# Units 0 to 3 of a delta-rule attention kernel: V summed in a PSUM bank instead of on VectorE, and four pieces' exponents made by ScalarE ahead of time

## The chip, the cores and the metric

The kernel runs on one core of a Trainium2 chip. The metric is device microseconds of one execution; a median over runs of the same program is given. The core has five instruction queues that matter here: TensorE (PE, matmuls into PSUM), VectorE (DVE), ScalarE (ACT), GpSimd (POOL) and SyncE (SP, which only issues DMAs). ScalarE and GpSimd issue a few DMAs too. Each works through its own instructions in program order and waits at semaphores for the others.

## The reference

Two blocks in a row. First a delta-rule attention over 4 batches x 8 heads, 768 steps, head dimension 48; then a feed-forward block on its 3072 rows of 384 features.

```python
k_n = k / (norm(k, axis=-1) + 1e-06)
for t in range(S):
    y[:, :, t] = einsum('bhd,bhde->bhe', q[:, :, t], state)
    v_old      = einsum('bhde,bhd->bhe', state, k_n[:, :, t])
    state     += beta[:, :, t] * outer(k_n[:, :, t], v[:, :, t] - v_old)
h = x @ w_in                       # 384 -> 2048
out = (h * sigmoid(1.702 * h)) @ w_out   # 2048 -> 384
```

q, k, v and beta arrive as 32-bit floats. The weights w_in and w_out arrive as 64-bit floats; the kernel reads them as pairs of 32-bit words and makes 32-bit floats of them with integer and float operations.

## The kernel before

**Units.** The sequence is cut into 6 chunks of 128 steps. The first chunk gives four units, 0 to 3, one for each batch; units 4 to 23 take two half chunks each (class Half). For a unit the recurrence becomes: a Gram matrix G = K K^T per head (gram_whole, line 475, for units 0 to 3), scores M = K Q^T (scores, 657), the triangular inverse of I + beta G in 32x32 diagonal blocks (invert, 543, on VectorE, for all of a chunk's units at once), a solve with it, and outputs and a state update (outputs, 768).

**The solve of units 0 to 3** goes over the four 32-row blocks of V. For each block, solve (716) multiplies V's block with the inverted diagonal block into psU, and solved (723) copies psU back over V as U, on ScalarE. Then below (703) multiplies Gram blocks with U into psR for every block further down, and rest (712) subtracts psR from V, on VectorE: for the first block in two instructions, rows 32 to 64 and the rest, for the others in one. together (1137) issues solves and belows of two units head by head in one burst. hops (1303) staggers two units so that one's solve runs beside the other's below: eight steps for units 0 and 1 (path), eight for 2 and 3 (later). warm(n) puts n matmuls without use on TensorE between the hops; put_out (1311) issues a unit's outputs and its state sum (line 766, ST<-psY,ST on VectorE).

**Conversion of the weights** is VectorE's work beside all this. conversion (224) is a generator. For one piece it does: mask the exponent (first operation, VectorE), rescale it (a Relu on ScalarE), put the sign in, mask the high mantissa, add the low word, multiply (four more on VectorE). pieces (249) gives the order: w_in in nine pieces, namely two halves of the first quarter (P0, P1), two of the second (P2, P3), three thirds of the third (P4 to P6), two halves of the last (P7, P8), 768 elements a partition each, but 512 for the thirds; then w_out in pieces of 384 or 768. conversions (275) overlaps neighbours: the next piece's first operation stands between the second and the third of the present one's, and its Relu is issued after it. fill(us) (322) pulls operations until their nominal costs (0.75, 0.95, 0.7, 0.95, 0.95) use up its budget; this writes VectorE's order by hand. After the piece of w_out that begins at block 6 the same stream goes on with the second inverse, invert(1), then with the rest of w_out. The last quarter of w_in is fetched into the place of P0 and P1, as soon as P1 is done (301), on SyncE's queue.

**The first inverse.** invert(0) runs on VectorE from 28.6 to 58.4 us. Beside it stand, in program order: the scores of units 0 to 3 (1285), the scaling of K of units 4 and 5 by 16 ScalarE instructions (next(scaling), 1290), their turns and Grams (1291 to 1294), then the rest of the inverse (1295). Its end puts 38 warming matmuls on TensorE (606) and sends the result through DRAM: stores Yd for units 0 and 1 on SyncE, for units 2 and 3 on ScalarE's queue (beside, 618), and loads XB for all four on SyncE (626). Behind them on SyncE: the diagonal blocks of units 4 and 5 (send_blocks), one piece of w_out, and inside the fill at 1301 the last quarter of w_in.

**After the solves** TensorE gets the feed-forward block: hidden (938), fed one step per hop from the fourth later hop on and then in the loop at 1382, together with fill(1.0); both_written (1084), which waits for converted w_out; and from unit 4 on slots (1186), in which the pending feed-forward work is spread between the small steps.

**PSUM** has eight banks: two for the feed-forward block (ps_moe), two "big", four "seq" until early_banks closes. A tile that takes a bank again waits for the readers of the tile before it.

```python
def rest(self, blk, psR):
    for u in (slice(BS, 2*BS), slice(2*BS, C)) if blk == 0 else (slice((blk+1)*BS, C),):
        vec.tensor_tensor(self.V[u], self.V[u], psR[u], op=ALU.subtract)
...
for i in range(2 * NB):
    together(*next(path))
    ...
    if 0 < i < 2 * NB - 1:
        fill(1.7)
```

Of the kernel before, what the change touches and what calls it, by code (L numbers as in the profile page):

```python
# [10 lines left out]
U32 = mybir.dt.uint32  # L11
AX = mybir.AxisListType
# [6 lines left out]
def kernel(  # L19
# [23 lines left out]
    C = 128  # L43
# [29 lines left out]
    ps_seq = early_banks.enter_context(tc.tile_pool(name="ps_seq", bufs=4, space=PSUM))  # L73
# [68 lines left out]
    bI = cpool.tile([128, BS], F32, name="bI")  # L142
    bL = cpool.tile([128, NC - 1, BS], F32, name="bL")
# [21 lines left out]
    pool.memset(low, -896.0 * (1 << 23))  # L165
    raws = w_out.rearrange("p f d -> p (f d)").bitcast(I32)
# [57 lines left out]
    def conversion(dst, raw, shape):  # L224
# [48 lines left out]
    done = set()  # L273

    def conversions():

        whole = list(pieces())

        def begin(i):
            dst, raw, shape, name = whole[i]  # L280
            ops = conversion(dst, places[name[1]] if raw is None else raw, shape)
            return ops, next(ops)
# [192 lines left out]
    def gram_whole(n):  # L475
# [7 lines left out]
        pool_, tag = (ps_seq, "seq") if c == 0 or n > DEEP + B else (ps_big, "big")  # L483
# [59 lines left out]
    def invert(c, b0=0, nb=B):  # L543
# [6 lines left out]
        tt(N, N, bc, op=ALU.mult)  # L550
# [88 lines left out]
    class Step:  # L639
# [62 lines left out]

        def below(self, blk, h, psR):
            r = slice(blk * BS, (blk + 1) * BS)
            for k in range(blk + 1, NB):
                u = slice(k * BS, (k + 1) * BS)
                pe.matmul(
                    psR[u, h, :], lhsT=self.G[r, h, u], rhs=self.U[r, h, :],
                    start=True, stop=True,
                )  # L710

        def rest(self, blk, psR):
            for u in (slice(BS, 2 * BS), slice(2 * BS, C)) if blk == 0 else (slice((blk + 1) * BS, C),):
                vec.tensor_tensor(self.V[u], self.V[u], psR[u], op=ALU.subtract)
# [24 lines left out]
        def queries(self):  # L739
            whole = [bank("psY", (128, 512)) for _ in range(2)]  # L740
# [396 lines left out]
    def together(solves, belows):  # L1137
# [4 lines left out]
        psRs = [bank("psR", big=blk == NB - 2 and len(belows) > 1) for X, blk in belows]  # L1142
# [106 lines left out]
    fetch_in(0, other_queue)  # L1249

# [15 lines left out]
    fetch_in(1, other_queue)  # L1266
    for b in range(B):
        load_values(b, sync)
    fetch_in(2)
# [15 lines left out]
    for s in pair:  # L1285
# [30 lines left out]
    path, later = hops(*pair[:2]), hops(*pair[2:])  # L1316
    for i in range(2 * NB):
# [31 lines left out]
    for i in range(1, 2 * NB):  # L1349
# [5 lines left out]
        fill(1.7)  # L1355
# [92 lines left out]
```

## Time and profile before

| | us |
|---|---|
| median of 3 runs | 719.43 (719.0 to 720.79) |
| profiled execution | 719.79 |
| its span, first to last instruction | 718.1 |
| PE / PEld busy | 673.8 / 580.2 |
| DVE busy | 464.8 |
| ACT / POOL busy | 232.8 / 252.3 |
| mean granted TensorE clock | 0.976 |

Times in the text are microseconds from the start of the span. A row of a timeline gives start, duration, engine, line, operation, output<-inputs by the program's names, shape, how many alike in a row, and in brackets how long the engine stood idle before it and who ended that. Most instructions carry line 122, where a helper records them: the names tell them apart. VU is V (and U over it), NT and YB the inverse's matrices, ph and po the two products of the feed-forward block, raw or w_out<-in_moe_w_in weights that are fetched (w_out's memory holds raw w_in for a while). A row with q behind the engine is a DMA issue by that queue. A busy TensorE is not TensorE at its peak, since a matmul's end is modelled.

| stretch | what runs |
|---|---|
| 0 to 28 | K, Grams of units 0 to 3, first piece of w_in |
| 28.6 to 58.4 | first inverse on VectorE |
| 64 to 84 | path: hops of units 0 and 1 |
| 83 to 109 | later: hops of units 2 and 3 |
| 101 to 149 | ph of the first rows; second inverse on VectorE from 123 to 154 |
| 161 to 718 | slots from unit 4 on |

### The profile page before, as it was taken

To read this page: it belongs to the slowest core of one execution; us is meant where nothing else is said; L and a number is where in the kernel's file an instruction comes from. 1 tells how busy PE (TensorE), PEld (TensorE's weight loads), DVE (VectorE), ACT (ScalarE), POOL (GpSimd) and SP (SyncE) were. 2 spreads that over 40 slices of the span, in tenths; PEclk is the share of its full clock that TensorE was granted. 3 is DMA by queue.
4 is the path that set the end of the run, shared out by engine and by line. 5 is a ranking of instruction groups with operands and counts; after the bars stand their busy time and mean duration, and the time that the engine had idled before them with its cause. 6 is when DMAs were issued, how large, how long until landed. Compare 5 with 4: busy or idle time off the path is not lost.

```text
span 718.1 us, 20437 instructions
## 1 busy us (share of the span) xinstructions
PE 673.8 (94%) x8779; PEld 580.2 (81%) x8779; DVE 464.8 (65%) x880; ACT 232.8 (32%) x553; POOL 252.3 (35%) x258
## 2 busy tenths in 40 slices
PE   9188899987999999999999999999999999999997
PEld 7156778853568888898988998988988988989997
DVE  5799988976577498597596695795893992110000
ACT  3362545433233313323333233323323223122020
POOL 6084003210256552552732633623522403304032
PEclk9577999999999999999999999999999999999999
DMA  9895845242222213214114123213122101000100
GB/s 169 143 187 112 215 126 134 56 79 81 57 52 60 57 37 79 42 37 94 29 37 92 31 57 73 46 44 60 33 53 57 29 24 32 8 23 2 28 0 23
DMA packets 129180, 46.66 MB, mean 65 GB/s; under 512 B 118849, under 2 KB 123585, under 8 KB 129089
## 3 DMA queue, kind: packets, MB, share of 16 engines
q1 hardware_dynamic: 125664, 40.94, 27.7%
q0 software_dynamic: 2240, 4.02, 2.8%
q8 instruction: 69, 1.13, 0.7%
q10 hardware_dynamic: 1184, 0.39, 0.2%
q14 instruction: 23, 0.18, 0.1%
HBM read 33.13 MB, written 11.01 MB: 61 GB/s over the span
## 4 chain that ended last, share of the span: by engine, by line
PE 52%; DVE 32%; DMA 7%; issue 4%; ACT 3%; SPq 2%; DVEq 0%; POOL 0%; ACTq 0%; POOLq 0%
PE ph L122 23%; PE po L122 17%; DVE P L122 12%; DVE YB L122 6%; PE four L122 4%; DVE NT L122 3%; DVE w_out L122 3%; DVE VU L122 3%; DMA NT<-Nd 2%; DMA Nd<-G 2%; PE psU L122 2%; PE psT L122 2%; PE ps_warm L122 2%; PE psR L122 2%; DVE w_in L122 1%
## 5 line engine op out<-in xcount | busy, mean ns | idle before, releaser
L122 PE MATMUL ph<-xT,w_in 128*128 128x256 f32 x1152 | 258.1, 381 | 0.2
L122 PEld LDWEIGHTS ph<-xT,w_in 128*128 128x128 f32 x1152 | 215.6, 190 | 30.6 <-DVE o L122 0.7
L122 PE MATMUL po<-w_out,gT 128*128 128x192 f32 (+1 forms) x720 | 139.7, 349 | 11.1 <-DVE w_out L122 5.4
L971 POOL TENSOR_TENSOR gT<-gT 128x512 f32<-128x512 f32 x80 | 105.1, 1323 | 103.6 <-ACT gT L122 68.4
L122 PEld LDWEIGHTS po<-w_out,gT 128*128 128x128 f32 x720 | 118.4, 191 | 25.5 <-DVE w_out L122 8.7
L122 DVE TENSOR_TENSOR P<-NT,YB 64x2 f32<-64x2 f32 (+9 forms) x200 | 121.4, 607 | 5.8
L122 ACT ACTIVATE gT<-ph 128x512 f32<-128x512 f32 x90 | 53.7, 597 | 144.9 <-PE ph L122 143.8
L122 DVE TENSOR_REDUCE YB<-P 64x2 f32<-64x2 f32 (+9 forms) x200 | 81.8, 409 | 6.9
L122 PE MATMUL po<-TW,gT 128*128 128x192 f32 x480 | 82.3, 328 | 1.1 <-ACT o L122 1.1
L122 PEld LDWEIGHTS po<-TW,gT 128*128 128x128 f32 x480 | 78.0, 190 | 2.4 <-ACT o L122 1.7
L122 ACT COPY VU<-psU 32x384 f32<-32x384 f32 x96 | 45.1, 470 | 58.5 <-PE psU L122 43.7
L839 POOL TENSOR_SCALAR_AFFINE_SELECT M<-M 64x512 f32<-64x512 f32 x40 | 30.0, 750 | 93.7 <-ACT M L122 91.7
L122 DVE TENSOR_TENSOR o<-o,po 128x192 f32<-128x192 f32 x40 | 13.9, 347 | 74.0 <-PE po L122 44.5
L122 DVE TENSOR_TENSOR VU<-VU,psR 32x384 f32<-32x384 f32 (+1 forms) x56 | 31.0, 554 | 41.7 <-PE psR L122 40.5
L122 DVE TENSOR_TENSOR NT<-NT,bL 64x1024 f32<-64x1024 f32 (+1 forms) x9 | 12.7, 1416 | 46.6 <-DMA NT<-Nd 46.6
L106 POOL DMA_DIRECT2D KN<-in_k_dram x24 | 17.1, 713 | 68.7 <-PE four L122 68.7
L122 DVE TENSOR_TENSOR VU<-VU,four 128x384 f32<-128x384 f32 x19 | 10.5, 551 | 45.7 <-issue 33.1
L122 PEld LDWEIGHTS psU<-VU,XB 32*32 32x32 f32 x1536 | 27.1, 105 | 15.0 <-issue 8.5
L341 POOL TENSOR_TENSOR rn<-ssq,half 128x8 f32<-128x8 f32 x12 | 22.2, 1849 | 45.7 <-DVE ssq L122 45.7
L122 ACT COPY xT<-four 128x256 f32<-128x256 f32 (+1 forms) x40 | 13.1, 328 | 74.5 <-DVE ST L122 72.1
L122 ACT COPY M<-four 128x512 f32<-128x512 f32 x19 | 11.1, 586 | 78.2 <-DVE VU L122 69.4
L122 PE MATMUL psU<-VU,XB 32*32 32x48 f32 x1536 | 32.0, 202 | 4.1 <-DVE VU L122 4.0
(123 smaller groups left out, 772.1 us busy)
## 6 DMA issues: line engine op xcount, KB each, us to landing
QP<-in_q_dram SPq DMA_DIRECT2D x40, 96.0 KB, 2.9
VU<-in_v_dram SPq DMA_DIRECT2D x40, 96.0 KB, 3.6
out_dram<-o SPq DMA_DIRECT2D x40, 96.0 KB, 2.2
raw<-in_moe_w_out_dram SPq DMA_DIRECT2D x9, 384.0 KB, 3.9
NT<-Nd SPq DMA_DIRECT2D x24, 128.0 KB, 2.4
XB<-Yd SPq DMA_DIRECT2D x24, 128.0 KB, 2.6
Yd<-NT SPq DMA_DIRECT2D x22, 128.0 KB, 2.2
Nd<-G SPq DMA_DIRECT2D x86, 32.0 KB, 1.7
```

The lines of the kernel that those rows point to most:

```text
L106: dma(out=place(dst, n)[rows, :, 0:D], in_=src[b, :, t, :].rearrange("h p d -> p h d"),)
L122: return lambda *a, **kw: tc.keep_in_program_order(op(*a, **kw))
L341: nc.gpsimd.tensor_tensor(rn, ssq, half, op=ALU.pow)
L839: nc.gpsimd.affine_select(out=M, in_=M, compare_op=ALU.is_gt, fill=0.0, base=0, pattern=[[0, H], [1, CH]], channel_multiplier=-1,)
L971: (engine or nc.gpsimd).tensor_tensor(o, a, b, op=op)
```

## The change

V of units 0 to 3 no longer lies in SBUF alone. gather starts a PSUM tile psV with V itself (a product with the identity); every below adds into it, for which the Gram is stored negated (bN, the negated beta, makes up for it in the first inverse); rest only copies the next 32 rows of psV to V, on ScalarE. The sixteen VectorE subtractions go, twelve ScalarE copies and four identity products come. The banks are dealt out anew: "seq" keeps two, two become "acc" (psV, and Grams and psY of odd units); psY of even units takes both of "seq".

For pieces P2 to P5 exponents makes the exponent on ScalarE alone, by three activations (Abs, a Relu on the upper 16 bits, a Relu), between the scores and after the Grams of units 4 and 5. The raw thirds of w_in are fetched ahead of V. In the hops the budgets and the warming are dealt out anew, and put_out of unit 0 comes after the last path hop.

```diff
-    ps_seq = early_banks.enter_context(tc.tile_pool(name="ps_seq", bufs=4, space=PSUM))
+    ps_seq = early_banks.enter_context(tc.tile_pool(name="ps_seq", bufs=2, space=PSUM))
+    ps_acc = early_banks.enter_context(tc.tile_pool(name="ps_acc", bufs=2, space=PSUM))
...
-        ts(p, hi, 0x7FF * E1, None, op0=AND)
-        yield 0.75
-        act.activation(p, p, ACT.Relu, scale=8.0, bias=low)
+        if early:
+            act.activation(dst, hi.bitcast(F32), ACT.Abs)
+            top = dst.bitcast(U16).rearrange("p j (n o) -> p j n o", o=2)[:, :, :, 1]
+            act.activation(p, top, ACT.Relu, scale=1.0 / 16, bias=floor)
+            act.activation(p, p, ACT.Relu, scale=float(1 << 23), bias=low)
+            yield 0.0
+        else:
+            ts(p, hi, 0x7FF * E1, None, op0=AND)
+            yield 0.75
+            act.activation(p, p, ACT.Relu, scale=8.0, bias=low)
...
+    def exponents(i):
+        if not whole:
+            whole.extend(pieces())
+        ops = conversion(*whole[i][0:3], True)
+        begun[i] = ops, next(ops)
...
-        pool_, tag = (ps_seq, "seq") if c == 0 or n > DEEP + B else (ps_big, "big")
+        pool_, tag = (ps_acc, "acc") if n % 2 else (ps_seq, "seq")
...
-        act.activation(G[:, 0::2], ps[0], ACT.Copy)
-        if B <= n < 2 * B + HB:
-            act.activation(G[:, 1::2], ps[1], ACT.Copy)
-        else:
-            vec.tensor_copy(G[:, 1::2], ps[1])
+        act.activation(G[:, 0::2], ps[0], ACT.Copy, scale=-1.0)
+        vec.tensor_scalar(G[:, 1::2], ps[1], -1.0, None, op0=ALU.mult)
...
-        tt(N, N, bc, op=ALU.mult)
+        tt(N, N, bc if c else bN.broadcast_to([np, BS, BS]), op=ALU.mult)
...
+        def gather(self):
+            self.psV = ps_acc.tile([128, H, D], F32, tag="acc", name="psV")
+            pe.matmul(
+                self.psV.rearrange("p h d -> p (h d)"), lhsT=ident, rhs=self.US[:, 0 : H * D],
+                start=True, stop=True, skip_group_check=True,
+            )
...
-                    psR[u, h, :], lhsT=self.G[r, h, u], rhs=self.U[r, h, :],
-                    start=True, stop=True,
+                    self.psV[u, h, :], lhsT=self.G[r, h, u], rhs=self.U[r, h, :],
+                    start=False, stop=True, skip_group_check=True,
...
-            for u in (slice(BS, 2 * BS), slice(2 * BS, C)) if blk == 0 else (slice((blk + 1) * BS, C),):
-                vec.tensor_tensor(self.V[u], self.V[u], psR[u], op=ALU.subtract)
+            u = slice((blk + 1) * BS, (blk + 2) * BS)
+            act.copy(self.V[u], self.psV[u])
...
-            whole = [bank("psY", (128, 512)) for _ in range(2)]
+            pool_, tag = (ps_acc, "acc") if self.n % 2 else (ps_seq, "seq")
+            whole = [pool_.tile([128, 512], F32, tag=tag, name="psY") for _ in range(2)]
...
+    pool.tensor_scalar(bN, bI, -1.0, None, op0=ALU.mult)
...
     fetch_in(1, other_queue)
+    fetch_in(2)
     for b in range(B):
         load_values(b, sync)
-    fetch_in(2)
...
         run(s.scored)
         warm(NA)
+        if s.n in (1, 3):
+            exponents(2 + s.n // 2)
     next(scaling)
...
     for n in (B, B + 1):
         gram(n)
+    for i in (4, 5):
+        exponents(i)
     run(inverting)
...
     path, later = hops(*pair[:2]), hops(*pair[2:])
+    for X in pair[:2]:
+        X.gather()
     for i in range(2 * NB):
         together(*next(path))
...
-        if i < 2 * NB - 2:
-            warm(NU if i == 2 else 2 * NU // 3)
-        if 0 < i < 2 * NB - 1:
-            fill(1.7)
-        if i == 2 * NB - 2:
-            put_out(pair[0])
+        if i < 2 * NB - 1:
+            warm(NU if i == 2 else NU // 2 if i in (1, 3, 4, 5) else 2 * NU // 3)
+        fill(2.2)
+    put_out(pair[0])
     load_diagonals(Ndx)
     together(*next(later))
-    fill(1.9)
     put_out(pair[1])
+    for X in pair[2:]:
+        X.gather()
...
-        fill(1.7)
+        fill(2.2)
```

More of the change, by code (lines that the diff above doesn't have):

```diff
@@ L11 @@
 U32 = mybir.dt.uint32
+U16 = mybir.dt.uint16
 AX = mybir.AxisListType
@@ L142 @@
     bI = cpool.tile([128, BS], F32, name="bI")
+    bN = cpool.tile([128, BS], F32, name="bN")
     bL = cpool.tile([128, NC - 1, BS], F32, name="bL")
@@ L165 @@
     pool.memset(low, -896.0 * (1 << 23))
+    floor = cpool.tile([128, 1], F32, name="floor")
+    pool.memset(floor, -15.0 / 32)
     raws = w_out.rearrange("p f d -> p (f d)").bitcast(I32)
@@ L222, in fetch_out, with conversion @@
         sync(out=as_rows(places[f])[:, 0], in_=moe_w_out[f * 128 : (f + 1) * 128, :])
-    def conversion(dst, raw, shape):
+    def conversion(dst, raw, shape, early):
         lo, hi = raw[:, :, :, 0], raw[:, :, :, 1]
@@ L273 @@
     done = set()
+    whole, begun = [], {}
+    def exponents(i):
[3 more added lines that the diff above has]
+        begun[i] = ops, next(ops)
     def conversions():
-        whole = list(pieces())
+        if not whole:
+            whole.extend(pieces())
         def begin(i):
+            if i in begun:
+                return begun[i]
             dst, raw, shape, name = whole[i]
-            ops = conversion(dst, places[name[1]] if raw is None else raw, shape)
+            ops = conversion(dst, places[name[1]] if raw is None else raw, shape, False)
             return ops, next(ops)
@@ L1141, in together @@
         psU = bank("psU") if solves else None
-        psRs = [bank("psR", big=blk == NB - 2 and len(belows) > 1) for X, blk in belows]
+        psRs = [bank("psR") if X.n >= B else None for X, blk in belows]
         for h in range(H):
```

## The prediction, on record before the changed kernel ran

> **What bounds the kernel now.** I read the page's slices first, then the timelines of the engines over the first 190 us, then the waits of TensorE.
>
> ```profile
> PE   9188899987999999999999999999999999999997
> DVE  5799988976577498597596695795893992110000
> ACT  3362545433233313323333233323323223122020
> PEclk9577999999999999999999999999999999999999
> ```
>
> A slice is 18 us. From the tenth on TensorE is full: nothing there gets shorter unless it starts earlier. Ahead of that VectorE is the fuller engine and ScalarE looks half empty, which is where the change puts its work. So the question is when TensorE reaches its dense stretch. Two rows of TensorE's timeline belong to it:
>
> ```profile
> 111.80 12.03 PE L122 MATMUL ph<-xT,w_in 128*128 128x256 f32 x55
> ...
> 151.25 9.94 PE L122 MATMUL po<-w_out,gT 128*128 128x384 f32 x30 [1.64 <-ACT TW L122]
> ```
>
> Unit 3's output matmuls end at 109.3. From there to the first solve of unit 4 at 161.1 TensorE has 51.8 us with 2.8 us of idle time (1.15 for kT, 1.64 in the row above). The second inverse ends on VectorE at 154.0, and its round trip (2.0 + 2.7 us of issues and a landing) takes it to about 160: both arrive together. **VectorE finishing sooner is therefore worth nothing by itself. The date that counts is 109.3.** After 161 TensorE waits for converted w_out:
>
> ```profile
> PE po L122 <- DVE w_out L122: 5.4, 4, 1.8
> ```
>
> **What it removes.** Sixteen VectorE operations VU<-VU,psR, 0.57 us each: 9.1 us. Four first conversion operations, two of 0.62 and two of 0.37: 2.0 us. VectorE has 11 us less before the second inverse. But the budgets of the hops grow: 8 x 2.2 in place of 6 x 1.7 in the first half. By the list of pieces (P0, P1 first quarter of w_in; P2, P3 second; P4 to P6 thirds; P7, P8 last) the first half's eight fills hold 24 operations: 7 of 0.97, 4 of 0.62, 9 of 0.71, 4 of 0.37, together 17.2 us. P7 now begins in hop 5's fill; before it began only after unit 2's first solve.
>
> **Hops.** A hop is a burst of solves and belows (0.87 on TensorE), then the two copies on ScalarE (0.47 each). Warming and turns run beside the copies. That makes about 2.2 us per hop, against 2.6 to 3.2 now, where VectorE's queue sets the pace.
>
> **ScalarE in the first inverse.** This I hold to be the step that decides.
>
> ```profile
> 47.92 1.20 ACT L122 COPY TW<-psQ 128x256 f32<-128x256 f32 x4 [0.80 <-PE psQ L122]
> 48.98 3.72 ACT L122 ACTIVATE KN<-KN,TW 128x48 f32<-128x48 f32 x16
> ...
> 56.96 0.66 ACT L122 ACTIVATE G<-psG 128x256 f32<-128x256 f32 x2 [1.22 <-PE psG L122]
> 58.46 0.84 ACTq L122 DMA_DIRECT2D Yd<-NT  x2
> ```
>
> The idle time in brackets is ScalarE waiting for TensorE, which waits for ScalarE: a chain through both, not free room. Its last link, G of unit 5, ends at 57.6. The Relu row of 128x768 takes 0.937, of 128x512 0.726. Abs and the 16-bit Relu are not in the trace; the bounds are 0.6 (the Relu row of 128x384) and 1.3 (the longest row of ScalarE here), and I take the Relu row of the same size, which is nearest. With 0.03 between dependent ones, P2 and P3 cost 2.9 each, P4 and P5 2.3 each. P2's words have their last issue at 37.8 and some 6.3 us to landing, so ScalarE, free at 43.7, starts at about 44.4. Units 2 and 3 then run 3.5 late, and what follows P3 6.5 late: G of unit 5 ends at 64.1. P4 and P5 end at 68.6, and only then does ScalarE issue the inverse's stores for units 2 and 3, now at 58.46. The trace has two table loads (1.28 us), the second for Gelu at 96.55; an Abs outside the set would add 1.3 to 2.6. [...]
>
> **TensorE at the start of the hops.**
>
> ```profile
> 55.52 1.40 PE L122 MATMUL psG<-kT 48*64 48x64 f32 x32 [0.48 <-ACT G L122]
> 57.29 6.76 PE L122 MATMUL ps_warm<-ident 128*128 128x256 bf16 x38 [0.37 <-DVE ps_warm L122]
> 63.97 0.86 PE L122 MATMUL psU<-VU,XB 32*32 32x48 f32 x16
> ```
>
> The 38 warming matmuls are queued behind unit 5's Gram: 63.4 in place of 56.9. They took 6.8 (0.18 each, 0.12 to 0.13 later at full clock) and may take 5 to 7. Then come two identity products of 384 columns, 0.7 each by the po rows. First solve at about 70, against 64.
>
> **SyncE.**
>
> ```profile
> 60.62 2.65 SPq L122 DMA_DIRECT2D XB<-Yd  x4
> 63.32 4.37 SPq L122 DMA_DIRECT2D Nd<-G  x8
> 67.74 1.72 SPq L122 DMA_DIRECT2D raw<-in_moe_w_out_dram  x1
> 69.55 6.82 SPq L122 DMA_DIRECT2D w_out<-in_moe_w_in_dram  x12
> ```
>
> Two of the four XB loads wait for ScalarE's stores: 68.6 + 0.4 + 2.6 to landing is 71.3. Behind them stand the blocks, one piece of w_out and the last quarter of w_in: 1.3 + 4.4 + 1.7 + 6.8, and 4.0 to landing: 89 (now 80).
>
> **VectorE and the banks.**
>
> ```profile
> 67.70 1.14 DVE L122 TENSOR_TENSOR VU<-VU,psR 32x384 f32<-32x384 f32 x2
> 84.23 0.36 DVE L122 TENSOR_TENSOR ST<-psY,ST 128x192 f32<-128x192 f32 x1
> 85.59 0.69 DVE L122 TENSOR_SCALAR w_in<-w_out 128x768 int32<-128x768 int32 x1
> 87.52 0.36 DVE L122 TENSOR_TENSOR ST<-psY,ST 128x192 f32<-128x192 f32 x1
> ```
>
> The third row is P7's first operation: in time, since its data were there at 80. In the changed order VectorE is there at about 83 (P6's Relu stands behind hop 4's copies on ScalarE, near 82) and waits to 89; P7's Relu stands in ScalarE's queue ahead of hop 6's copies, so these wait too. From P7's first operation to unit 0's state sum stand 0.62 + 1.42 + 0.97 + 0.62 + 0.62 + 1.94 + 0.97 + 0.62 + 0.30 = 8.1 us: the sum ends at about 97, not 84.6. Now the banks. Unit 0's psY takes both seq banks, and unit 2's first psU takes the first of them, which that sum still reads: a new wait, with all of TensorE's queue behind it. So unit 2's first solve is at 97; unit 1's sum ends at about 99.9, and the products that start psV of units 2 and 3 need its bank: 1.4 more, 101.3. Now this point is at 86.1: **+15.2.**
>
> Second half: hops 1 and 2 with 12 warming matmuls 2.35 each, hop 3 3.2 (warming and six ph), three of 2.4, the last 2.3, outputs and ph 1.55 + 1.5 + 1.55: 22.0, against 23.2 (86.1 to 109.3). **-1.2.**
>
> **Dense stretch.** The second inverse now begins six feeding steps earlier than in the order before, so VectorE no longer lags, and I count the 2.8 us of idle as gone (0 to 2.8): **-2.8.**
>
> **Slots 3 and 4.** VectorE enters with one small piece more done (2.4 us) and still sets the pace there: **-2.4**, between 0 and the 5.4 of the waits.
>
> **Costed at nothing.** The thirds of w_in go ahead of V on SyncE: 12 issues (6.9 us) and 4 (6.1) in the same stretch from 38 to 51. V then lands near 57 (5.2 after its last issue), the first product needs it near 69; without that cover the product would wait. Twelve VU copies move to ScalarE (5.6 us), counted in the hops; the belows are as many as before. Scores and whole Grams lose banks (seq has 2, not 4), but ScalarE empties the former tile of each before the next comes; otherwise a copy of 0.3 to 0.6 shows. The Gram's sign (0.69 on VectorE, 0.60 on ScalarE by the present evictions) and bN on GpSimd (ahead of needs at 28.6) cost nothing; if not covered, some tenths.
>
> **Sum.** 15.2 - 1.2 - 2.8 - 2.4 = +8.8. The profiled execution took 719.79 (span 718.1), 0.36 over the median of 719.43; 719.43 + 8.8 = **728.2**. From the unknown prices: Abs and the 16-bit Relu at 0.6 take 1.9 off, the slots at their other end 3.0; at 1.3, with table loads or slow warming, they add 3 to 4, and idle time that stays 2.8: 724 to 733.
>
> **Rivals.**
> *Faster: ScalarE takes the exponents in its idle time.* First solve at 65.4 (64 and the two products), hop 7 over at 83, no wait for P7, and VectorE early enough at unit 0's sum that unit 2 starts at 85; the second half ends at 105.5: -3.8 - 2.8 - 2.4 = -9, 710.5. For it: ScalarE's 3 to 5 tenths. Against it: the two-way chain above, and VectorE, which leaves the fill before the hops at about 67.3 and needs 17.2 + 1.9: unit 0's sum at 86.7 at the earliest. With that alone (*no change*) it is +3.1 - 2.8 - 2.4 = -2, 717.4 to 720.
> *Slower by less: ScalarE late, SyncE not held up* (P7's data at 83): unit 0's sum at 91.6, 5.4 us less, 723.
> *Slower by more: the clock.* TensorE would stand still for some 8 us from 83. In this trace the granted clock is 0.5 from 21 to 42, after the stop at 20, and again from 52 to 62. Half clock for one such 10 us stretch adds up to 5 us: 733. [...]
>
> **Chances.** Forecast 0.47 (724 to 733); clock 0.11; SyncE free 0.11; no change 0.09; faster 0.22, since two prices on ScalarE are unseen and a queue order may differ from my reading. By over 0.3% (2.2 us, about what a measurement of this kernel can tell): faster 0.22, within 0.09, slower 0.69. The range, 713 to 735, leaves out the lower half of the faster case and the end of the clock's. The forecast's own is 724 to 733.
>
> **What would show it.** G of unit 5 on ScalarE near 64; the first solve near 70; ScalarE's Yd issues near 69; a wait of VectorE's first P7 operation for in_moe_w_in; a wait of psU for ST near 97; hops of 2.2 us; unit 3's outputs ending near 123; the w_out waits below 5.4. I am wrong if the first solve stays near 65, or if unit 2's first solve comes before 85.

## The result, and the profile after

The changed kernel takes **738.71 us** (median of 4 runs, 736.92 to 741.16) against 720.11 for the kernel before in the same series: a ratio of 1.0261, 95% interval 1.0226 to 1.0296. It is slower by 18.6 us. The forecast was 728.2, range 713 to 735: the sign held, the size did not. The profiled execution took 741.16, the longest of the four, with a span of 739.5; against the 718.1 of before the trace therefore has 21.4 us to explain. Ratios in this document compare mean times, and that of f1_noexp_budgets leaves out one execution (733.27) that lies over 1.5% above that kernel's fastest.

The slices of the page, in the rows shown for before (a slice is now 18.5 us):

```profile
PE   9178897998899999999999999999999999999997
...
DVE  4799444995747659579399399398596693010000
ACT  3356535444234323332322413313323222222120
...
PEclk9667777999999999999999999999999999999999
```

ScalarE's fourth slice is fuller (6 against 2), and VectorE's fifth to seventh have fallen to 4: it waits. The clock row shows 6 and 7 in the second to seventh slice, where before has one 5 and two 7s. The clock's record puts TensorE at half clock from 84.0 to 101.0 and from 114.7 to 124.9, inside the hops; before had full clock from 62.3 to 171.6. Beside the early exponents there is one more, from 46.4 to 53.3, where before has full clock up to 52.1.

These dates tell where the time came from (start of the first TensorE instruction of each kind, or the end where it says so):

| us | before | after | added so far |
|---|---|---|---|
| G of unit 5 ends (ScalarE) | 57.6 | 65.65 | 8.0 |
| first solve | 64.0 | 71.4 | 7.4 |
| seventh path hop | 79.7 | 86.6 | 6.9 |
| last quarter of w_in has landed | 79.6 | 89.1 | 9.5 |
| unit 0's ST ends | 84.6 | 97.3 | 12.7 |
| first solve and below of units 2 and 3 together | 86.0 | 103.1 | 17.1 |
| unit 3's outputs end | 109.4 | 133.7 | 24.3 |
| first solve of the slots | 161.1 | 184.9 | 23.8 |
| end | 718.1 | 739.5 | 21.4 |

ScalarE's timeline after, for the rows that were shown before:

```profile
44.13 0.90 ACT L124 ACTIVATE w_in<-w_out 128x768 f32<-128x768 f32 x1 [0.21 <-DMA gT<-in_moe_w_in_dram]
45.12 0.93 ACT L124 ACTIVATE w_in<-w_in,floor 128x768 int32<-128x768 uint16 x1
...
64.99 0.66 ACT L124 ACTIVATE G<-psG 128x256 f32<-128x256 f32 x2 [1.22 <-PE psG L124]
...
69.15 0.80 ACTq L124 DMA_DIRECT2D Yd<-NT  x2
```

The first two are P2's Abs and 16-bit Relu; its last Relu follows at 46.09 with 0.94. The third is G of unit 5, which before began at 56.96. The last is the issue that stood at 58.46. SyncE's timeline:

```profile
60.23 11.89 SPq L124 DMA_DIRECT2D XB<-Yd  x4
...
77.69 9.43 SPq L124 DMA_DIRECT2D w_out<-in_moe_w_in_dram  x12
...
101.44 4.48 SPq L124 DMA_DIRECT2D xT<-last  x6
...
108.05 1.09 SPq L124 DMA_DIRECT2D raw<-in_moe_w_out_dram  x2
```

The four XB loads took 2.65 us of SyncE before and take 11.89 now: SyncE stands in the middle of them for ScalarE's stores. The last row matters later. VectorE:

```profile
89.09 0.69 DVE L124 TENSOR_SCALAR w_in<-w_out 128x768 int32<-128x768 int32 x1 [5.27 <-DMA w_out<-in_moe_w_in_dram]
...
96.92 0.35 DVE L124 TENSOR_TENSOR ST<-psY,ST 128x192 f32<-128x192 f32 x1
...
113.78 0.36 DVE L124 TENSOR_SCALAR w_out<-raw 128x384 int32<-128x384 int32 x1 [10.69 <-DMA raw<-in_moe_w_out_dram]
```

P7's first operation waits to 89.1 and unit 0's state sum ends at 97.3, as forecast. The third row is a wait that the forecast does not have. TensorE:

```profile
71.40 0.86 PE L124 MATMUL psU<-VU,XB 32*32 32x48 f32 x16
...
83.79 0.23 PE L124 MATMUL psV<-VU,gT 32*32 32x48 f32 x1 [1.36 <-issue]
...
96.79 1.48 PE L124 MATMUL psU<-VU,XB 32*32 32x48 f32 x16 [0.64 <-ACT xT L124]
...
101.64 1.56 PE L124 MATMUL psV<-VU,ident 128*128 128x384 f32 x4 [0.64 <-ACT xT L124]
...
109.06 1.46 PE L124 MATMUL ph<-xT,w_in 128*128 128x256 f32 x6
115.83 0.28 PE L124 MATMUL psU<-VU,XB 32*32 32x48 f32 x1 [5.32 <-ACT VU L124]
...
117.26 2.93 PE L124 MATMUL ph<-xT,w_in 128*128 128x256 f32 x6
```

Here the clock can be read from the work itself: sixteen solves take 0.86 at 71 and 1.48 at 97, six ph matmuls 1.46 at 109 and 2.93 at 117. The second row is a pause in the middle of a hop's burst, 1.36 us long, for which the trace names no releaser ("issue"); the clock falls right behind it, at 84.0. Its second fall, at 114.7, comes in the wait of the sixth row, which begins at 110.5. The fourth row is the four products that start psV of units 2 and 3; they wait for ScalarE's copies of unit 1's outputs. The waits from 60 to 140 (us in total, times, longest):

```profile
DVE w_out L124 <- DMA raw<-in_moe_w_out_dram: 10.7, 1, 10.7
ACT w_out L124 <- DVE w_out L124: 7.6, 2, 7.0
PE psU L124 <- ACT VU L124: 7.0, 2, 5.3
```

They are one chain: a fill in the later hops makes VectorE ask for w_out's second piece. Its fetch stands on SyncE at 108.05, behind unit 1's outputs (xT<-last). VectorE waits 10.7, the Relu that depends on it stands in ScalarE's queue and waits 7.0, ScalarE's copies of U stand behind the Relu, and TensorE waits 5.3 for them.

### The profile page after: what moved, and what is told of

The parts are those of the page before. It is cut to its first block, busy times and chain, and to the rows that moved or that the text cites. A ratio compares the mean times of both kernels' runs of the same rounds, so it can differ in the third digit from the quotient of the medians.

```text
span 739.5 us, 20460 instructions
## 1 busy us (share of the span) xinstructions
PE 690.5 (93%) x8787; PEld 592.4 (80%) x8787; DVE 454.7 (61%) x860; ACT 244.8 (33%) x573; POOL 253.5 (34%) x260
## 4 chain that ended last, share of the span: by engine, by line
PE 55%; DVE 23%; DMA 8%; ACT 4%; SPq 4%; issue 4%; POOL 1%; DVEq 0%; ACTq 0%; POOLq 0%
PE ph L124 22%; PE po L124 17%; DVE P L124 10%; DVE YB L124 5%; PE four L124 4%; SPq L124 3%; PE psU L124 3%; PE ps_warm L124 3%; DVE NT L124 3%; PE psT L124 2%; DMA w_out<-in_moe_w_in_dram 2%; DVE VU L124 2%; DMA NT<-Nd 2%; DVE w_out L124 2%; PE psR L124 1%
## 5 line engine op out<-in xcount | busy, mean ns | idle before, releaser
L124 PE MATMUL ph<-xT,w_in 128*128 128x256 f32 x1152 | 260.9, 384 | 0.5 <-ACT TW L124 0.5
L124 DVE TENSOR_REDUCE YB<-P 64x2 f32<-64x2 f32 (+9 forms) x200 | 81.7, 409 | 6.9
L867 POOL TENSOR_SCALAR_AFFINE_SELECT M<-M 64x512 f32<-64x512 f32 x40 | 30.4, 761 | 90.1 <-ACT M L124 88.0
L124 DVE TENSOR_TENSOR o<-o,po 128x192 f32<-128x192 f32 x40 | 13.8, 346 | 73.4 <-PE po L124 44.1
L124 PEld LDWEIGHTS psU<-VU,XB 32*32 32x32 f32 x1536 | 30.4, 108 | 20.3 <-issue 11.2
L124 DVE TENSOR_TENSOR VU<-VU,psR 32x384 f32<-32x384 f32 x40 | 22.1, 554 | 39.6 <-PE psR L124 38.9
L124 PE MATMUL psU<-VU,XB 32*32 32x48 f32 x1536 | 35.9, 207 | 7.7 <-ACT VU L124 7.0
L108 POOL DMA_DIRECT2D KN<-in_k_dram x24 | 17.1, 712 | 69.0 <-PE four L124 69.0
L124 DVE TENSOR_TENSOR VU<-VU,four 128x384 f32<-128x384 f32 x19 | 10.5, 551 | 45.9 <-issue 32.9
L364 POOL TENSOR_TENSOR rn<-ssq,half 128x8 f32<-128x8 f32 x12 | 22.2, 1847 | 46.7 <-DVE ssq L124 46.7
L124 ACT COPY M<-four 128x512 f32<-128x512 f32 x19 | 11.1, 586 | 78.0 <-DVE VU L124 69.2
```

Source lines behind the costliest of these rows:

```text
L108: dma(out=place(dst, n)[rows, :, 0:D], in_=src[b, :, t, :].rearrange("h p d -> p h d"),)
L124: return lambda *a, **kw: tc.keep_in_program_order(op(*a, **kw))
L364: nc.gpsimd.tensor_tensor(rn, ssq, half, op=ALU.pow)
L867: nc.gpsimd.affine_select(out=M, in_=M, compare_op=ALU.is_gt, fill=0.0, base=0, pattern=[[0, H], [1, CH]], channel_multiplier=-1,)
```

## The experiments

Accounts on trial: **lateness** (ScalarE's exponents delay everything behind them), **the next wait** (VectorE, entitled to more by the grown budgets, asks for data or a Relu that is not there, and the Relu holds up the hops' copies), **the clock** (TensorE at half speed in the hops), and **the banks** (unit 2 waits for unit 0's psY). The expectations call lateness theory 1, the sum in PSUM with its banks theory 2 and the clock theory 3. Medians of before ran from 720.1 to 721.3 in these series; each ratio is against its own.

**Each half of the change alone.** a1_noexp is the change without the two loops that call exponents; a2_exponly is before with conversion's early branch, those calls and the earlier fetch_in(2), and V still summed on VectorE.

```diff
 a1_noexp (against after)
-        if s.n in (1, 3):
-            exponents(2 + s.n // 2)
...
-    for i in (4, 5):
-        exponents(i)
```

> The changed kernel without the early exponents (P2 to P5 are converted as before; V in PSUM, banks and budgets stay as changed). Theory 1, ScalarE's queue in the first inverse is the cause: G of unit 5 back near 57.6, first solve near 65.5 (64 and the two identity products), ScalarE's Yd issues near 58.5, the last quarter of w_in landed near 80 and no wait for it; gathering of units 2 and 3 near 91 instead of 101.6, outputs of unit 3 ending near 115 instead of 133.7; time 719 to 724. Theory 2, the sum in PSUM and the new banks are the cause: the hops stay as slow, time 732 to 738.

> The kernel before with nothing but the early exponents of P2 to P5 and the thirds of w_in fetched ahead of V (V stays in SBUF, budgets and banks as before). Theory 1: first solve near 70, last quarter of w_in landed near 89, hops of 2.6 to 3.2 us behind it; w_in's P7 begins only after unit 2's first solve (near 91), so no wait for it; time 724 to 730. Theory 2: within 2 us of the kernel before.

Measured: a1_noexp 731.05, ratio 1.0132 (1.0086 to 1.0179); a2_exponly 733.36, 1.0193 (1.0163 to 1.0222). Neither lies in its expected range. The exponents alone cost 13 us and the V sum as written 11 us, and both together 18.6. In a2_exponly everything from the first solve (72.1, +8.1) through unit 3's outputs (118.7, +9.3) to the slots (171.8, +10.7) is late by about what ScalarE lost at the start. In a1_noexp the first solve is nearly in time (64.8) and the loss lies in the hops: 64.8 to 98.8 for what takes 64.0 to 86.0 before, at half clock from 75.2 to 99.1. Of that, the stretch from the seventh path hop to the first burst of units 2 and 3 takes 16.0 us (82.8 to 98.8), nearly the 16.5 of after and against 6.4 before, without any wait for w_in's data.

**Which exponents.** b3_exp23 keeps only P2 and P3 (between the scores), b4_exp45 only P4 and P5 (after the Grams of units 4 and 5).

```diff
 b3_exp23 (against after)
-    for i in (4, 5):
-        exponents(i)
```

> The changed kernel with only P2 and P3 made early (between the scores); P4 and P5 as before. Theory 1: G of unit 5 still near 65, first solve near 70.5, ScalarE's Yd issues near 65.7 (behind G, no longer behind P4 and P5), last quarter of w_in landed near 85 to 86; time 733 to 738.

> The changed kernel with only P4 and P5 made early (after the Grams of units 4 and 5); P2 and P3 as before. Theory 1: G of unit 5 near 57.3, first solve near 65, ScalarE's Yd issues near 61.5 to 62 (4.4 us of activations behind G), last quarter landed near 82 to 83; time 728 to 733, close to the run without early exponents. If any exponent on ScalarE is what costs: 735 to 738.

Measured: b3_exp23 737.54, 1.0229 (1.0197 to 1.026); b4_exp45 730.16, 1.013 (1.0093 to 1.0167), the same as a1_noexp, both as expected. The six activations inside the chain between ScalarE and TensorE carry the cost; the six behind it look free here. They are free only beside the other losses (f2_best_exp45, below).

**One hold-up at a time.** a3_yd_sp puts the inverse's stores of units 2 and 3 on SyncE, so they no longer wait for ScalarE; a4_fetch issues w_out's second piece ahead of unit 1's outputs; d1_all_three does both and warms with 12 matmuls after every path hop; b1_fetch_warm is a4_fetch with more warming.

```diff
 a3_yd_sp
-                (beside if c == 0 and b >= HB else dma)(
+                dma(
 a4_fetch
     put_out(pair[0])
+    fetch_out(1)
...
-    for f in range(1, 3):
-        fetch_out(f)
+    fetch_out(2)
 b1_fetch_warm (against a4_fetch; in d1_all_three: warm(NU))
-            warm(NU if i == 2 else NU // 2 if i in (1, 3, 4, 5) else 2 * NU // 3)
+            warm(40 if i == 5 else NU)
```

> The changed kernel with the inverse's stores Yd of units 2 and 3 on SyncE's queue instead of ScalarE's. Theory 1 in its SyncE part: SyncE's loads XB of units 2 and 3 no longer wait to 71, the last quarter of w_in lands near 81, VectorE's 5.3 us wait for it and ScalarE's 3.8 us wait go; the first solve stays near 71. Gathering of units 2 and 3 near 97 instead of 101.6; time 4 to 7 us under the changed kernel, 732 to 735. If SyncE's hold-up does not matter: unchanged, 738.

> The changed kernel with the fetch of w_out's second piece (fetch_out(1)) issued right after unit 0's outputs instead of behind unit 1's outputs and their six transfers. If the 10.7 us wait of VectorE at 113.8 for that piece, with ScalarE's Relu behind it ahead of the copies of the hop, is what lengthens the second half: that wait falls below 2 us, ScalarE's 7.0 and TensorE's 5.3 us waits go, the second half takes 23 to 26 us instead of 30.5, time 731 to 734. If half clock alone lengthens it: second half still 28 or more, time 737 or more.

> The run with the early fetch of w_out's second piece, and more warming matmuls in the first half: 12 after every path hop, 40 after hop 5, where TensorE stands still behind the wait for the last quarter of w_in (6, 8 or 12 before). Theory 3, besides the queues half clock lengthens the hops: the 20 us of half clock from 90 to 110 disappear or shrink below 8 us, the second half's front (unit 2's and 3's bursts and outputs) shortens, time 729 to 732 against 735.9. If the clock does not matter: 735 to 738, or longer by the added matmuls.

> The changed kernel with the three hold-ups behind the first solve taken away: Yd of units 2 and 3 on SyncE, w_out's second piece fetched behind unit 0's outputs, 12 warming matmuls after every path hop. Only ScalarE's lateness before the first solve is left. Theories 1 and 3 together: first solve still near 71, no half clock after 70, units 2 and 3 gathered near 96, unit 3's outputs ending near 120, time 726 to 730. If something else in the sum costs, it stays above 732.

Measured: a3_yd_sp 736.5 (1.0229, 1.0188 to 1.027), a4_fetch 735.91 (1.0223, 1.0208 to 1.0239), b1_fetch_warm 735.6 (1.0201, 1.0171 to 1.0232), d1_all_three 733.31 (1.0175, 1.0152 to 1.0198). All four missed their first range: the gains came out smaller than expected. Each hold-up is real, but taking one away lowers the median by 2 to 3 us and all three by 5.4, because another takes its place; for a3_yd_sp (732.6 to 739.6, beside 736.9 to 741.2 of after) not even that is clear of the spread. In a3_yd_sp the last quarter lands at 81.8 in place of 89.1, and then (waits from 62 to 135):

```profile
DVE w_in L124 <- ACT w_in L124: 12.8, 3, 9.9
DVE w_out L124 <- DMA raw<-in_moe_w_out_dram: 9.3, 1, 9.3
```

VectorE now waits 9.9 for a Relu of P6 that stands in ScalarE's queue among the hops' copies, about as long as it waited in after for the same Relu (5.4) and then for the data (5.3). b1_fetch_warm has the better clock, 0.967 to 0.974 against 0.955 to 0.958 in a4_fetch, and is no faster: by its profiled execution the stretch from the seventh hop to the first burst of units 2 and 3 falls from 19.6 to 10.1, but the hops with their added matmuls take 18.6 in place of 13.7. d1_all_three, with all three mended, stays above 732, the bound of its expectation for "something else"; its waits in the same window:

```profile
DVE w_in L124 <- ACT w_in L124: 10.2, 1, 10.2
...
DVE w_out L124 <- DMA raw<-in_moe_w_out_dram: 5.6, 1, 5.6
```

The wait for raw is again there, shorter: it is for the piece after.

**The V sum, arranged otherwise.** b2_noexp_warm is a1_noexp with 12 warming matmuls in every path hop; c2_big is b2_noexp_warm with psY of even units in the "big" banks, so unit 2 need not wait for unit 0's state sum. c1_best is a1_noexp with several things moved at once: the gathers of units 0 and 1 ahead of the rest of the inverse, the old warming, 30 warming matmuls ahead of the hops, psY in "big", unit 0's outputs and w_out's second fetch after the seventh hop. c3_before_warm is before with the change's warming (6 in four hops).

```diff
 c2_big (against b2_noexp_warm; also in c1_best)
-            pool_, tag = (ps_acc, "acc") if self.n % 2 else (ps_seq, "seq")
+            pool_, tag = (ps_acc, "acc") if self.n % 2 else (ps_big, "big")
 c1_best (against a1_noexp, further)
-    NW, NR, NA, NY, NU = 80, 11, 3, 38, 12
+    NW, NR, NA, NY, NU = 80, 11, 3, 30, 12
...
+    for X in pair[:2]:
+        X.gather()
     run(inverting)
...
-            warm(NU if i == 2 else NU // 2 if i in (1, 3, 4, 5) else 2 * NU // 3)
+            warm(NU if i == 2 else 2 * NU // 3)
...
+        if i == 2 * NB - 2:
+            put_out(pair[0])
+            fetch_out(1)
 c3_before_warm (against before)
-            warm(NU if i == 2 else 2 * NU // 3)
+            warm(NU if i == 2 else NU // 2 if i in (1, 3, 4, 5) else 2 * NU // 3)
```

> The run without early exponents, with 12 warming matmuls after every path hop (6, 8 or 12 before), nothing else. Theory 3: half clock from 75 to 99 goes, hops take 2.2 to 2.7 us, unit 2's second burst comes near 90 instead of 98.8, time 721 to 725 against 731. If the slow hops of that run come from the copies on ScalarE or the banks: hops stay near 3.5 us at full clock, 729 to 732.

> The run without early exponents and with 12 warming matmuls, and psY of units 0 and 2 in the big banks, so that unit 2's first psU does not take the bank that unit 0's state sum reads. If the bank wait of the prediction is real: unit 2's first solve 1 to 3 us earlier against unit 0's outputs, time 1 to 3 us lower than that run (725 to 731 in its four executions). If not: the same.

> V in PSUM without early exponents, arranged after what the runs showed: the products that start psV of units 0 and 1 ahead of the inverse's warming (30 instead of 38 matmuls), 8 warming matmuls per hop as in the kernel before (12 after hop 2), outputs of unit 0 after the seventh hop as before with psY in the big banks, w_out's second piece fetched right behind them. If the sum in PSUM can pay at all, it is here: first solve near 64, units 2 and 3 gathered near 87, unit 3's outputs ending near 110 to 112, time 717 to 722. If hops at 2.2 us cost the clock (theory 3): half clock in the first half again, 723 to 728.

> The kernel before with the warming of the first half dealt out as in the changed one (6 instead of 8 matmuls after hops 1, 3, 4 and 5; nothing else). Theory 3, the clock hangs on these matmuls: half clock somewhere between 75 and 110, 2 to 6 us slower. If two matmuls a hop do not matter: within 1.5 us of the kernel before, clock full from 62 on.

Measured: b2_noexp_warm 728.08 (1.0104, 1.0068 to 1.014), c2_big 730.8 (1.0124, 1.0088 to 1.0161), c1_best 724.49 (1.0056, 1.0036 to 1.0075), c3_before_warm 720.55 (0.9999, 0.9983 to 1.0014). Unit 0's bank falls: in c2_big unit 2's first solve no longer waits (0.64 in b2_noexp_warm), and the median is no lower. The wait of psV's products for unit 1's bank (0.64) was left in every run. b2_noexp_warm lies above both ends of its expected 721 to 725; c1_best lies in its second range, but without the half clock that this range was given for (its profiled execution has full clock from 62.3 to 175.0). Two warming matmuls fewer per hop, by themselves, do nothing either. b2_noexp_warm keeps full clock through the hops: its stretch from the seventh path hop to the first burst of units 2 and 3 takes 10.1 us, against 16.0 in a1_noexp with the same order. That difference is the clock's price in this stretch. But its path hops take 2.7 us, since TensorE now has the warming to do, so part of the gain is spent.

**The budgets.** e1_budgets is after with the old budgets of the fills, f1_noexp_budgets the same without exponents, e2_best17 is c1_best with them.

```diff
-        fill(2.2)
+        if 0 < i < 2 * NB - 1:
+            fill(1.7)
...
     together(*next(later))
+    fill(1.9)
...
-        fill(2.2)
+        fill(1.7)
```

> The changed kernel with the fill budgets of the kernel before (1.7 in six hops of the first half and in the second, 1.9 after unit 2's first solve); everything else as changed. If the grown budgets are the common cause of the late-data waits: VectorE's 5.3 us wait for the last quarter of w_in and its 10.7 us wait for w_out's second piece fall below 3 us together, first solve still near 71, units 2 and 3 gathered near 96, unit 3's outputs ending near 121, time 728 to 732. If not: waits of the same size at other pieces, 735 to 739.

> The arranged kernel without early exponents (724.5) with the budgets of the kernel before. VectorE has 9 us less to do in the hops, so ScalarE's 8.6 us of waits for its first operations shrink and the hops come closer to 2.2 us: time 719 to 723, at best level with the kernel before. If the two pairs of products and the copies on ScalarE cost by themselves: 723 to 726 again.

> The change without the early exponents, as in a1_noexp (731.1), but with the old budgets of the fills (1.7, and 1.9 after unit 2's first solve) and nothing else rearranged. If the grown budgets are what the V sum costs as it was written: path hops of about 2.4 us at full clock, unit 3's outputs ending at 110 to 113, 721 to 725. If the order of gathers, warming and put_out costs it (c1_best had those mended too): unit 3's outputs at 117 to 121 and 728 to 731.

Measured: e1_budgets 738.57 (1.0252, 1.0207 to 1.0297), f1_noexp_budgets 723.27 (1.0054, 1.0016 to 1.0093), e2_best17 722.74 (1.0019, 0.9994 to 1.0044). Without exponents the grown budgets are most of the V sum's cost: in the profiled executions seven hops take 15.1 us in place of a1_noexp's 18.0 (at half clock from 75.2). What is left in f1_noexp_budgets is 0.5%, and in e2_best17 nothing that can be told from before. With exponents the old budgets change nothing, so e1_budgets met its second expectation (735 to 739), and the reason is found in the last pair.

**Both halves in the best arrangement.** f2_best_exp45 is e2_best17 with the exponents of P4 and P5, f3_best_exp with all four.

```diff
 f2_best_exp45 (against e2_best17)
+    for i in (4, 5):
+        exponents(i)
     run(inverting)
```

> e2_best17 (722.7: the V sum rearranged, old budgets, no exponents) with the early exponents of P4 and P5 alone, behind the Grams of units 4 and 5. If these two cost nothing (b4_exp45 against a1_noexp): 720 to 723, at best 1.2 us under e2_best17 for the two first operations that VectorE loses; ScalarE's Yd issue moves from 57.9 to about 61 and the first solve stays under 64. If ScalarE's late Yd issues cost here, where nothing else is late: first solve at 65 or later, last quarter landed over 82, 726 or more.

> f2_best_exp45 with the exponents of P2 and P3 between the scores as well, so the whole intention of the change with the arrangement that costs the V sum nothing. If the exponents of P2 and P3 cost what they cost alone (a2_exponly, +13): first solve at 71 to 72, last quarter landed at 89 to 92, 733 to 737. If most of a2_exponly's cost came from the old V path on VectorE: unit 3's outputs end by 116 and 726 to 729.

Measured: f2_best_exp45 725.95 (1.0077, 1.0057 to 1.0097), f3_best_exp 731.97 (1.0191, 1.0122 to 1.026). So P4 and P5 cost 3.2 us once nothing else is late: ScalarE's Yd issue goes from 57.9 to 61.2, the first solve from 62.7 to 64.2, the slots from 161.7 to 167.0. Not all of this is lateness, for this profiled execution has half clock from 79.2 to 86.1; the median lies just under the second expectation (726 or more). f3_best_exp falls between its two expected ranges, with two executions near one and two in or above the other. Its profiled execution shows lateness nearly by itself, for it had full clock from 69.2 on: the first solve at 71.7 against 62.7 in e2_best17, the slots at 170.7 against 161.7, the span 727.5 against 719.1. Nine us lost at the first solve arrive as nine at the slots and 8.4 at the end (in between they shrink to 7.6, since e2_best17 has 3.4 us of half clock in its hops). The Relu wait is there too (f3_best_exp, VectorE):

```profile
86.85 0.69 DVE L124 SCALAR_TENSOR_TENSOR w_in<-gT,w_in 128x512 int32<-128x512 int32 x1 [9.41 <-ACT w_in L124]
```

and the path hops still run at 2.2 us beside it (71.7, 73.4, 75.7, 78.0, 80.2, 82.6); from the seventh hop to the first burst of units 2 and 3 it takes 9.8 us (86.0 to 95.8). e1_budgets has the same wait:

```profile
87.59 0.69 DVE L124 SCALAR_TENSOR_TENSOR w_in<-gT,w_in 128x512 int32<-128x512 int32 x1 [11.03 <-ACT w_in L124]
```

but half clock from 86.8 to 107.3, and the same stretch takes 15.8 (86.6 to 102.4). The clock row of e1_budgets' page:

```profile
PEclk9566859999999999999999999999999999999999
```

and of f3_best_exp's:

```profile
PEclk9576999999999999999999999999999999999999
```

The 8 in the fifth slice and the 5 in the sixth of e1_budgets are the hops, where f3_best_exp has 9. So VectorE's long wait alone does not make the hops long.

**The clock, over all executions.** Each execution's mean granted clock is known, and in f1_noexp_budgets and f3_best_exp the long executions are the ones with the low clock:

| kernel | executions, us (mean clock) |
|---|---|
| f1_noexp_budgets | six at 720.0 to 724.4 (0.973 to 0.981), four at 728.4 to 733.3 (0.959 to 0.967) |
| f3_best_exp | 728.5, 729.2 (0.974), 734.8 (0.967), 739.0 (0.955) |
| a1_noexp | 725.3 (0.972), 731.0 to 731.8 (0.960 to 0.970) |
| after | 736.9 to 741.2 (all four 0.953 to 0.956) |
| e1_budgets | 737.9 to 741.9 (all four 0.955 to 0.958) |
| before, beside f1 | 718.5 to 722.3 (0.973 to 0.981) |

The code of a row is the same throughout, and one row spans up to 13 us. f3_best_exp at 0.974, as in its profiled execution without half clock in the hops, takes 728.5 and 729.2, the forecast's number; with a mean clock of 0.955 it takes 739.0, which is what after and e1_budgets take in every execution.

## Why the prediction was right in sign and wrong in size

**ScalarE at the start: right.** Forecast and measured: G of unit 5 at 64.1 and 65.65, Yd issue 69 and 69.15, first solve 70 and 71.4, last quarter 89 and 89.06, P7's wait to 89 and 89.09, unit 0's ST 97 and 97.27. (The forecast's 68.6 + 0.4 + 2.6 is 71.6 and not 71.3, and the ends that it lists, 1.9 + 3.0 down and 4 + 2.8 up, make 723 to 735 rather than 724 to 733; neither decides anything.) The price taken for the unseen activations, the Relu row of the same size, was right within 0.06 us. G of unit 5 came 1.5 later than forecast, and the half clock from 46.4 to 53.3 lies in that stretch; what it cost there no run shows. No table load came: the trace still has two (1.28 us each, at 0.80 and 118.27), and none stands beside Abs or the two Relus. f3_best_exp shows that 9 us lost here reach the end as 8.4, about the forecast's +8.8. That the totals agree is partly luck, for the terms do not: against before, its profiled execution has +9.8 up to units 2 and 3 (15.2 were forecast), -1.7 in the second half, +1.4 in the dense stretch (-2.8 were forecast) and -0.2 in the slots.

**Up to units 2 and 3: the date nearly right, by luck.** +15.2 was forecast, +17.1 measured. The forecast reached it by P7's data and unit 0's bank. P7's wait is in the trace, and TensorE waits 1.73 for the copies behind P7's Relu; but a1_noexp has no wait for P7's data and takes as long from the seventh hop on (16.0 and 16.5). The wait for unit 0's sum that was forecast is not there: unit 2's first solve starts at 96.79, ahead of that sum (96.92), after 0.64 of waiting for ScalarE's xT, and c2_big shows no gain without it. At full clock the same order takes 10.1 (b2_noexp_warm; d1_all_three, with all exponents, 90.0 to 100.1, the same). So about 6 of the 17.1 us are the clock. Another 3.7 stand at full clock too, for before takes 6.4 there: in the changed order unit 0's outputs part unit 1's last solve from unit 2's first, which were one burst, the warming behind the seventh hop is new (1.05 for eight), and psV's products come behind unit 1's outputs (0.64 and 1.56), the one part of this that the forecast had, with 1.4.

**The step that failed: "Second half ... 22.0".** It took 30.6 (103.1 to 133.7), 7.2 more than before, where the forecast booked 1.2 less. Without its two disturbances the term is right: 21.7 in f3_best_exp, and 22.2 in a1_noexp, where VectorE's wait for raw (4.7) does not reach TensorE. The first disturbance is the wait for w_out's second piece, whose issue stands behind unit 1's outputs on SyncE. The forecast followed SyncE's queue up to the last quarter of w_in and stopped there; the grown budgets take VectorE past that, into pieces whose fetches are still to be issued. With the fetch ahead (a4_fetch) this half takes 23.4 (105.5 to 128.9); but there the half clock lasts from 89.9 to 110.3, the stretch ahead takes 19.6, and the median falls by only 2.8. The second disturbance is the half clock from 114.7 to 124.9, which begins inside that wait. b3_exp23 shows this step by itself: its profiled execution keeps full clock from 65.7 to 106.7, takes 10.2 from the seventh hop to the first burst of units 2 and 3, and then 30.4 for the second half, with half clock from 106.7 to 116.9 and, from 60 to 140, the same chain of waits:

```profile
DVE w_out L124 <- DMA raw<-in_moe_w_out_dram: 6.5, 1, 6.5
...
PE psU L124 <- ACT VU L124: 4.7, 1, 4.7
```

**The rival "slower by more: the clock" happened, on top of the forecast's lateness.** It was priced at 5 us for one stretch of 10, with a chance of 0.11. In the hops 27.3 us ran at half clock (17.1 and 10.2), and the mean clock (0.953 to 0.956) says that it was alike in every execution. 738.71 - 728.2 = 10.5 is also what lies between executions of f3_best_exp with high and low mean clock (10.5, from 728.5 to 739.0) and of f1_noexp_budgets (about 9, between its two groups). The forecast held the clock for an alternative, though its own likeliest case already had TensorE standing still in the hops; here it came beside the forecast's dates and not in place of them. What makes the clock fall, and behind how long a pause, no run shows. In before it fell at 21.4, inside a stop of 15.56, and at 171.6, behind pauses of 1.32 and 1.81. In after the second fall in the hops came 4.2 us into the wait of 5.32, and the first behind a pause of 1.36 in thinly filled hops; and e2_best17 fell to half clock from 76.3 to 79.7 behind

```profile
76.04 0.20 PE L124 MATMUL psU<-VU,XB 32*32 32x48 f32 x1 [1.61 <-issue]
```

f1_noexp_budgets kept its clock in the profiled execution (mean 0.973) with such a pause of 1.4, so the pause alone does not decide.

**Dense stretch: -2.8 forecast, -0.5 measured.** From unit 3's outputs to the slots it takes 51.2 us against 51.7. Three short waits for ScalarE remain (0.46, 0.90 and 0.97), where the forecast had counted all idle time as gone.

**Slots: right.** From their first solve to the end 554.6 against 557.0, the -2.4 that was forecast. TensorE's wait for converted w_out fell from 5.4 to:

```profile
PE po L124 <- DVE w_out L124: 2.9, 3, 1.1
```

**Hops of 2.2 us: right for the first five** (71.4, 73.2, 75.3, 77.5, 79.5, 81.7). The pause and the clock then take it back: seven hops take 15.2 us against 15.7 before. In e2_best17 they take 16.5, by such a pause and a 3.4 us stretch of half clock, and unit 3's outputs end at 109.9 against 109.4. The V sum, which takes 9 us of subtractions from VectorE, gains nothing even there: against before, e2_best17 has -1.3 at the first solve, +0.9 in the hops, +2.7 from the seventh hop to the first burst of units 2 and 3 (the new warming and psV's products, as above), and -1.7 in the second half.

**Sum in the profiled execution**, by the table: first solve +7.4, seven hops -0.5, on to units 2 and 3 +10.2, second half +7.2 (30.6 against 23.4), dense stretch -0.5, slots -2.4: +21.4.

**What stays open.** What lets the clock fall in one execution of f1_noexp_budgets or f3_best_exp and not in the next is not shown, nor is what TensorE waits for in the "issue" pauses (last section). Since no experiment could set the clock, the split between stalls that bring the half clock and stalls that it lengthens is read from pairs of kernels, not measured by itself. d1_all_three, whose clock was mostly mended (0.966 to 0.976), still took 733.3, some 5 us above f3_best_exp at 0.974; its waits are shown, their single prices are not.

## What to carry to other kernels

An engine that looks half empty can still be the slower side of a chain that goes to and fro with another engine. Ask of each added instruction whether the chain passes it, and count the DMAs that the engine issues behind it: here 10 us of activations in "idle" time moved the first solve by 7 to 9 (a1_noexp to after, e2_best17 to f3_best_exp), and the end by about as much. If the likeliest case makes TensorE stand still or work thinly, the price of the clock (here 27.3 us of half clock in the hops) belongs into the sum, and not into a rival beside it. When a budget of filler work is raised, follow the queues to the last datum that the larger budget reaches, for the wait stands there, and a helper's activation that waits for it holds up everything behind it on ScalarE (in after a Relu that waited 7.0, and TensorE 5.3 for the copies behind it).

## What was not expected of the hardware

- Abs from every second 32-bit word, Relu from the upper 16 bits of a word and a plain Relu take nearly the same time in after: 0.90, 0.93 and 0.94 for 128x768; 0.67 to 0.73 for 128x512.
- One program on one core spans 720.0 to 733.3 (f1_noexp_budgets) with the mean granted clock between 0.959 and 0.981, while before stays within 718.5 to 722.3 beside it. The half-clock stretches differ in length too: 3.4 us in e2_best17 (76.3 to 79.7), 6.8, 17.1 and 10.2 in after (from 46.4, 84.0 and 114.7), 20.5 in e1_budgets (86.8 to 107.3) and 23.9 in a1_noexp (75.2 to 99.1).
- TensorE pauses with no releaser in the trace stand inside single bursts: 1.36 in after (to 83.79) and 1.61 in e2_best17 (to 76.04). The waits of TensorE between 60 and 140 us have such "issue" pauses in seven more kernels with the V sum in PSUM, the longest from 0.9 (c2_big) to 2.2 (a3_yd_sp); those of a1_noexp (64 to 100) and of before (64 to 92) have none. What TensorE waits for in them no run shows.
- In b2_noexp_warm warming mended the clock and spent much of the gain: with 12 matmuls in every hop there is no half clock in its hops, but they take 2.7 us against 2.2 in f3_best_exp. b1_fetch_warm (735.6, mean clock 0.967 to 0.974) is level with a4_fetch (735.9, 0.955 to 0.958).
